# An attention and MLP block on one core: the softmax maxima turned on VectorE, a max product in the filling's bank, a constant lead and idle products in the tail

## The chip, the core and the metric

The kernel runs on one core of a Trainium2 chip. Its engines work beside each other: TensorE (PE in the profile, with its weight loads as PEld), VectorE (DVE), ScalarE (ACT), GpSimd (POOL), and SyncE (SP), which issues most of the transfers. The time is device microseconds of one execution; of the kernel before there are three runs and one profiled execution.

## The reference, cut to what matters

A transformer block with modulation by a condition vector: layer norm, attention of 32 query heads over one shared key and value head (S = 2048, D = 512, Dh = 16), a gated residual, a second layer norm and a gelu MLP (F = 1376) with another gated residual.

```python
mod = (silu(c) @ w_mod).reshape(1, 6, 1, -1)
sa, ca, ga, sb, cb, gb = (mod[:, i] for i in range(6))
h = layernorm(x) * (1 + ca) + sa
q = heads(h @ wq); k = h @ wk; v = h @ wv          # 32 heads of q, one k, one v
p = softmax(q @ k.T * Dh ** -0.5)
x = x + ga * ((p @ v) @ wo)
h = layernorm(x) * (1 + cb) + sb
x = x + gb * (gelu(h @ w1 + b1) @ w2 + b2)
```

The softmax is taken with the row maximum subtracted; all inputs are float32.

## The kernel before, in words

**Tiles.** The 2048 rows are 8 blocks of 256 rows. A block has 8 units of 4 heads, so there are 64 units. The 4 heads of a unit lie in two groups of 64 rows of the array (s = 0 and 1), two heads (j = 0 and 1) in each.

**Two passes.** Every unit's scores are computed twice. In the max pass (class `Max`) a product m of 64 x 128 queries with 512 keys goes to one of three PSUM banks (tag "m"), and VectorE reduces it to its maximum (L455); 32 of these make a unit. When the last is done, a further reduce (L463) gives the maxima mm, 128 queries by 8. Two ticks or more later `put_max` turns mm with a TensorE transpose (L475) into one more use of tag "m", ScalarE copies it to SBUF (L479), GpSimd splits it in two parts mh and ml (lines L117 and L122, in the helper `split`), and four small DMAs write these parts as two more rows of the unit's query tile qst (`send`). In the exp pass (`sexp`) the product e of keys and qst has the maximum subtracted by those rows, and ScalarE takes the exponential (L506). It needs one of four banks: e0, e1, e2, or "x". `pv` multiplies the exponentials by v into the unit's accumulator (acc, L517): 16 matmuls of the trace for one call.

**Order.** The instructions' order on each engine is the order in which the program issues them, written out by hand. The main loop runs over units u and, in each, over K = 0, 2, 4, 6. One such iteration has two half-steps, and each ends with one `pv`: 512 half-steps in all. A half-step issues four max products and four exp products and, if there is any, filling work: a half of a batch of the matmuls of other stages (late query projections, the output projection and MLP of the block before). Filling accumulates in bank "x" (its matmuls have the helper lines L165 and L171). If there is none, `plain` issues the half-step (called unfilled below; 84 of the 512). In an unfilled half-step the four exp products have the banks 1, 2, 0 and x, in the order `(K, 0, a)`, `(K, 0, b)`, `(K, 1, c)`, `(K, 1, d)` of their arguments; on TensorE the order comes out as m, m, e (bank 1), e (2), m, e (x), e (0), m. `holder` says that a batch that isn't finished holds "x"; no unfilled half-step has one.

**Due times.** `clock` counts four ticks for an iteration (one ahead of each `due()`); `later(n, fn)` issues fn at the `due()` n ticks on. `lead` says how many max products shall be done by each unit: 6 iterations' worth ahead (LEAD), and from 3 (LEAD_0) up to that over the first 8 units, which puts ten max products in place of eight into six of the early iterations.

**The rest of a block.** `rest` and `rest_steps` issue what follows a block's attention: the output projection (wops), add to x (L680), statistics (L687), normalization, transposes (tp2), modulation, the two MLP matmuls (w1ps, w2ps) and gelu. For seven blocks it is filling, for the last one (`fast`) it is the tail.

Of the kernel before, what the change touches and what calls it, by code (L numbers as in the profile page):

```python
# [9 lines left out]
F32 = mybir.dt.float32  # L10
# [12 lines left out]
LEAD = 6  # L23
LEAD_0 = 3
# [8 lines left out]
AHEAD = 0.75  # L33

# [6 lines left out]
def adaln_mqa_mlp(  # L41
# [189 lines left out]
    load_x(3)  # L231
    qbufs = [att.tile([P, 2, HQ], F32R, name=f"qst{i}") for i in range(QBUFS)]
# [191 lines left out]
    class Max:  # L424
# [17 lines left out]
        def step(self, s):  # L442
# [7 lines left out]
            m = psum.tile([P, 512], F32, name=f"m{u}_{j}_{t}_{kc}_{s}", tag="m", bufs=3)  # L450
# [9 lines left out]
            if self.left[u] == 0:  # L460
                put_at[u] = clock[0] + 2
                mm = att.tile([P, 4 * T], F32, name=f"mm{u}", tag="mm", bufs=2)
                nc.vector.tensor_reduce(out=mm, in_=self.mx.pop(u), axis=AX.X, op=ALU.max)  # L463
                maxima[u] = mm

    maxima = {}

    def put_max(u):

        w = blocks[units[u][0]][1]  # L470
        T = w // P
        qst = qsts[u]
        mm = maxima.pop(u)
        pt = psum.tile([P, 512], F32, name=f"mt{u}", tag="m", bufs=3)
        nc.tensor.transpose(pt[:4 * T, :P], mm, ident)  # L475
# [3 lines left out]
        nc.scalar.copy(m32, pt[:4 * T, :P])  # L479
# [13 lines left out]
    def sexp(u, K, j, s, bank):  # L493

        w = blocks[units[u][0]][1]
        qst = qsts[u]
        if (u, K) not in ptiles:
            ptiles[u, K] = att.tile([P, 2, 2, 512], F32, name=f"p{u}_{K}", tag="p", bufs=3)
# [21 lines left out]
    def finish_unit(u):  # L520
# [13 lines left out]
        if b == len(blocks) - 1:  # L534
# [56 lines left out]
    def rest(b, fast):  # L591
# [55 lines left out]
        ready = {}  # L647
        w1ts = {}
        later(*((5, lambda: norm(0)) if fast else (2, fetch)))
        return rest_steps(b, fast, rp, bank, ons, ready, w1ts)  # L650

    def rest_steps(b, fast, rp, bank, ons, ready, w1ts):
# [6 lines left out]
        for hf in range(w // HQ):  # L659
# [3 lines left out]
            x1 = rp.tile([P, 2, D], F32, name=f"x1_{b}_{hf}", tag="x1", bufs=2)  # L663
            xh = rp.tile([P, 2, D], F32, name=f"xh2_{b}_{hf}", tag="xh2", bufs=1)
            nc.sync.dma_start(out=x1, in_=xf[row0 + hf * HQ:row0 + (hf + 1) * HQ, :].rearrange("(t p) d -> p t d", p=P))
# [649 lines left out]
```

## Time and profile before

| | us |
|---|---|
| median of three runs | 1652.74 |
| lowest and highest | 1651.8, 1653.97 |
| the profiled execution, its own time | 1652.54 |
| its span in the trace | 1650.7 |
| PE busy | 1607.0 (97%) |
| DVE busy | 1418.3 (86%) |
| ACT busy | 1222.0 (74%) |
| POOL busy | 609.1 (37%) |

The granted TensorE clock was 0.995 in the mean. The span leaves out 1.84 us around it. Busy time of PE holds what a matmul waits inside its queue, so the shares say less than the single rows do: in a row of the timeline stand the start, the busy time, engine, line, operation, output and inputs with their shapes, how many instructions the row groups, and in brackets the idle time ahead of it and what released it.

### The profile page before, as it was taken

To read this page: it belongs to the slowest core of one execution; us is meant where nothing else is said; L and a number is where in the kernel's file an instruction comes from. 1 tells how busy PE (TensorE), PEld (TensorE's weight loads), DVE (VectorE), ACT (ScalarE), POOL (GpSimd) and SP (SyncE) were. 2 spreads that over 40 slices of the span, in tenths; PEclk is the share of its full clock that TensorE was granted. 3 is DMA by queue.
4 is the path that set the end of the run, shared out by engine and by line. 5 is a ranking of instruction groups with operands and counts; after the bars stand their busy time and mean duration, and the time that the engine had idled before them with its cause. 6 is when DMAs were issued, how large, how long until landed. Compare 5 with 4: busy or idle time off the path is not lost.

```text
span 1650.7 us, 41301 instructions
## 1 busy us (share of the span) xinstructions
PE 1607.0 (97%) x16371; PEld 1028.5 (62%) x16371; DVE 1418.3 (86%) x2433; ACT 1222.0 (74%) x2445; POOL 609.1 (37%) x894
## 2 busy tenths in 40 slices
PE   6999999999999999999999999999999999999988
PEld 4455644456666676656666576656766576656657
DVE  7788999999988998899988998999988998899524
ACT  4356777778877887778877787778877787778843
POOL 6235246424611363124601363124601363124702
PEclk9999999999999999999999999999999999999998
DMA  7244321212112130212112030212112030122122
GB/s 263 80 121 159 130 75 53 86 38 77 57 49 75 28 105 15 78 46 80 57 47 76 28 107 16 64 58 81 54 45 78 30 108 15 49 80 87 52 107 92
DMA packets 80157, 121.59 MB, mean 74 GB/s; under 512 B 15497, under 2 KB 53001, under 8 KB 79965
## 3 DMA queue, kind: packets, MB, share of 16 engines
q1 hardware_dynamic: 79852, 118.96, 22.0%
q8 instruction: 129, 2.11, 0.5%
q14 instruction: 64, 0.52, 0.1%
q0 software_dynamic: 112, 0.01, 0.0%
HBM read 91.13 MB, written 27.26 MB: 72 GB/s over the span
## 4 chain that ended last, share of the span: by engine, by line
PE 85%; DVE 8%; issue 2%; ACT 1%; DMA 1%; POOL 1%; SPq 0%; DVEq 0%; POOLq 0%; ACTq 0%
PE acc L517 29%; PE m L452 25%; PE e L505 15%; PE w1ps L171 6%; DVE mx L455 6%; PE w2ps L171 3%; PE w1ps L165 1%; PE w2ps L165 1%; PE wops L171 1%; ACT p L506 1%; PE mt L475 1%; PE kps L147 1%; PE qps L171 1%; PE tp L171 1%; DVE st L687 1%
## 5 line engine op out<-in xcount | busy, mean ns | idle before, releaser
L455 DVE TENSOR_REDUCE mx<-m 128x1 f32<-128x512 f32 x2048 | 1279.4, 683 | 145.9 <-PE m L452 115.1
L506 ACT ACTIVATE p<-e 128x512 f32<-128x512 f32 x2048 | 1070.7, 599 | 292.6 <-PE e L505 223.8
L452 PE MATMUL m<-ks,qst 64*128 64x512 f32 x2048 | 838.3, 433 | 12.8 <-DVE mx L455 4.2
L505 PE MATMUL e<-qst,ks 64*128 64x512 f32 x2048 | 700.3, 399 | 2.7 <-DMA qst<-ml 2.6
L517 PE MATMUL acc<-p,va 128*32 128x256 f32 x8192 | 548.0, 385 | 0.0
L452 PEld LDWEIGHTS m<-ks,qst 64*128 64x128 f32 x2048 | 358.6, 183 | 274.7 <-DVE mx L455 181.5
L505 PEld LDWEIGHTS e<-qst,ks 64*128 64x128 f32 x2048 | 359.0, 184 | 41.4 <-ACT p L506 19.3
L517 PEld LDWEIGHTS acc<-p,va 128*32 128x32 f32 x8192 | 213.8, 109 | 218.8 <-issue 116.7
L171 PE MATMUL w1ps<-h2H,w1t 64*128 64x256 f32 x1232 | 235.1, 287 | 0.0
L117 POOL TENSOR_SCALAR mh<-m 8x128 fp32r<-8x128 f32 x64 | 18.4, 288 | 450.7 <-ACT m L479 448.8
L171 PEld LDWEIGHTS w1ps<-h2H,w1t 64*128 64x128 f32 x1232 | 184.1, 185 | 0.0
L171 PE MATMUL w1ps<-h2L,w1t 64*128 64x256 f32 x616 | 169.5, 275 | 0.0
L171 PE MATMUL w2ps<-w2H,gL 64*128 64x512 f32 x282 | 115.7, 410 | 0.0
L171 PE MATMUL w2ps<-w2L,gH 64*128 64x512 f32 x282 | 115.5, 410 | 0.0
L171 PE MATMUL w2ps<-w2H,gH 64*128 64x512 f32 x282 | 115.3, 409 | 0.0
L171 PEld LDWEIGHTS w1ps<-h2L,w1t 64*128 64x128 f32 x616 | 113.6, 184 | 0.0
L780 POOL TENSOR_SCALAR tt<-tt 128x256 f32<-128x256 f32 x77 | 31.2, 405 | 177.2 <-DVE mx L455 96.3
L122 POOL TENSOR_TENSOR gL<-z,gH 128x256 fp32r<-128x256 f32 x88 | 66.0, 750 | 20.0 <-DVE gH L121 13.6
L781 POOL TENSOR_TENSOR tt<-tt,z 128x256 f32<-128x256 f32 x77 | 56.7, 737 | 6.4
L791 POOL TENSOR_TENSOR z<-tt,z 128x256 f32<-128x256 f32 x77 | 56.2, 729 | 6.0
L790 POOL TENSOR_TENSOR tt<-tt,z 128x256 f32<-128x256 f32 x77 | 56.2, 730 | 0.0
L171 PEld LDWEIGHTS w2ps<-w2H,gH 64*128 64x128 f32 x282 | 52.0, 184 | 0.6
(183 smaller groups left out, 1443.6 us busy)
## 6 DMA issues: line engine op xcount, KB each, us to landing
w1t<-dw SPq DMA_DIRECT2D x82, 512.0 KB
qst<-dq SPq DMA_DIRECT2D x384, 32.0 KB
do<-oc SPq DMA_DIRECT2D x64, 128.0 KB
dw<-w1s SPq DMA_DIRECT2D x11, 512.0 KB
xt<-in_A_x_dram SPq DMA_DIRECT2D x4, 1024.0 KB
wml<-in_w_mod_dram SPq DMA_DIRECT2D x8, 512.0 KB
dq<-qH SPq DMA_DIRECT2D x16, 256.0 KB
dq<-qL SPq DMA_DIRECT2D x16, 256.0 KB
```

The lines of the kernel that those rows point to most:

```text
L122: eng_l.tensor_tensor(out=dst_l, in0=src, in1=raw(dst_h), op=ALU.subtract)
L165: nc.tensor.matmul(ps, a, b_, start=first_, stop=last_)
L171: nc.tensor.matmul(ps, a[rows], b_[rows], start=first_ and s == 0, stop=last_ and s == 1)
L452: nc.tensor.matmul(m, qsts[u][rows, j, t * P:(t + 1) * P], ks[rows, kc * 512:(kc + 1) * 512], start=True, stop=True)
L455: nc.vector.tensor_reduce(out=self.mx[u][:, i, kc:kc + 1], in_=m, axis=AX.X, op=ALU.max)
L505: nc.tensor.matmul(e, ks[rows, kt * P:(kt + 1) * P], rhs, start=True, stop=True)
L506: nc.scalar.activation(ptiles[u, K][:, j, s, :], e, AF.Exp, scale=0.25)
L517: nc.tensor.matmul(accs[u][32 * cidx:32 * cidx + 32, :], va[:, kt, :], rhs, start=kt == 0, stop=kt == NKT - 1)
L780: nc.gpsimd.tensor_scalar(out=tt, in0=tt, scalar1=1.0, scalar2=1.0, op0=ALU.mult, op1=ALU.add)
L781: nc.gpsimd.tensor_tensor(out=tt, in0=tt, in1=z, op=ALU.mult)
L790: nc.gpsimd.tensor_tensor(out=tt, in0=tt, in1=z, op=ALU.mult)
L791: nc.gpsimd.tensor_tensor(out=z, in0=tt, in1=z, op=ALU.add)
```

## The change

What it does, part by part:

- **Maxima.** At a unit's last max product VectorE reduces into one of two constant tiles `mms` of 128 x 32 (zeroed at the start), and turns it with four transposes of 32 x 32 into mt (32 x 128). GpSimd's split reads mt one tick later, and the four DMAs are issued three ticks after the last maximum (`MAX_WAIT`). TensorE's transpose, ScalarE's copy and `put_some` go; 64 of each.
- **Unfilled half-steps.** `plain` puts the last max product of the row group t into bank "x", and the exp products have the banks 1, 2, 0, 1 (first half-step) and 2, 0, 1, 2 (second).
- **Lead.** 3 iterations' worth, without a ramp.
- **Loads.** x and the first three tiles of w1 of the last block are loaded by `fetch_rest` at the end of its last unit but one; for other blocks where they were. Statistics, normalization and what follows come one tick later.
- **Tail.** `stir` issues 4, 8 and 4 idle products of 128 x 512 into "x" ahead of the transposes of the second layer norm and the modulation.

```diff
-LEAD = 6
-LEAD_0 = 3
+LEAD = 3
+MAX_WAIT = (1, 3)
+STIR = (4, 8, 4)
...
+    mms = [const.tile([P, 32], F32, name=f"mm{i}") for i in range(2)]
+    for mm in mms:
+        nc.gpsimd.memset(mm, 0.0)
...
-        def step(self, s):
+        def step(self, s, **place):
             u = self.at[s]
             if u not in self.items:
                 self.begin(u)
...
             j, t, kc = self.items[u][s].pop(0)
             if not self.items[u][s]:
                 self.at[s] += 1
-            m = psum.tile([P, 512], F32, name=f"m{u}_{j}_{t}_{kc}_{s}", tag="m", bufs=3)
+            m = psum.tile([P, 512], F32, name=f"m{u}_{j}_{t}_{kc}_{s}", **(place or dict(tag="m", bufs=3)))
             rows = slice(64 * s, 64 * s + 64)
             nc.tensor.matmul(m, qsts[u][rows, j, t * P:(t + 1) * P], ks[rows, kc * 512:(kc + 1) * 512],
                              start=True, stop=True)
...
             if self.left[u] == size[u] // 2 and u and u + 1 < NU:
                 load_q(u + 1)
             if self.left[u] == 0:
-                put_at[u] = clock[0] + 2
-                mm = att.tile([P, 4 * T], F32, name=f"mm{u}", tag="mm", bufs=2)
-                nc.vector.tensor_reduce(out=mm, in_=self.mx.pop(u), axis=AX.X, op=ALU.max)
-                maxima[u] = mm
-    maxima = {}
-    def put_max(u):
-        w = blocks[units[u][0]][1]
-        T = w // P
+                put_max(u, self.mx.pop(u))
+    placed = set()
+    def put_max(u, mx):
+        T = blocks[units[u][0]][1] // P
         qst = qsts[u]
-        mm = maxima.pop(u)
-        pt = psum.tile([P, 512], F32, name=f"mt{u}", tag="m", bufs=3)
-        nc.tensor.transpose(pt[:4 * T, :P], mm, ident)
+        mm = mms[u % 2]
+        nc.vector.tensor_reduce(out=mm[:, :4 * T], in_=mx, axis=AX.X, op=ALU.max)
+        mt = att.tile([32, P], F32, name=f"mt{u}", tag="mt", bufs=2)
+        for g in range(0, P, 32):
+            nc.vector.transpose(out=mt[:, g:g + 32], in_=mm[g:g + 32, :])
         mh = att.tile([4 * T, P], F32R, name=f"mh{u}", tag="mh", bufs=2)
         ml = att.tile([4 * T, P], F32R, name=f"ml{u}", tag="ml", bufs=2)
-        m32 = att.tile([4 * T, P], F32, name=f"m32_{u}", tag="m32", bufs=2)
-        nc.scalar.copy(m32, pt[:4 * T, :P])
-        split(mh, ml, m32, nc.gpsimd, nc.gpsimd)
         def send():
             for s in range(2):
                 for r, src in ((48, mh), (49, ml)):
                     dst = qst[64 * s + r:64 * s + r + 1].rearrange("p j (t n) -> p (j t) n", n=P)
                     nc.sync.dma_start(out=raw(dst), in_=raw(src[2 * T * s:2 * T * (s + 1), :].unsqueeze(1)))
-        later(2, send)
+            placed.add(u)
+        later(MAX_WAIT[0], lambda: split(mh, ml, mt[:4 * T], nc.gpsimd, nc.gpsimd))
+        later(MAX_WAIT[1], send)
...
+            if Q == NQ - 2:
+                assert stage[b - 1] == 1
+                later(2, lambda: fetch_rest(b))
...
+    def fetch_w1(b, w1ts, f):
+        w1ts[f] = wts_pool["rest"].tile([P, 2, KD, P], F32R, name=f"w1t{b}_{f}", tag="w1t", bufs=3)
+        nc.sync.dma_start(out=raw(w1ts[f]), in_=dw1[f])
+    def fetch_rest(b):
+        row0, w = blocks[b]
+        x1 = wts_pool["rest"].tile([P, 2, D], F32, name=f"x1_{b}", tag="x1", bufs=2)
+        nc.sync.dma_start(out=x1, in_=xf[row0:row0 + w, :].rearrange("(t p) d -> p t d", p=P))
         w1ts = {}
-        later(*((5, lambda: norm(0)) if fast else (2, fetch)))
-        return rest_steps(b, fast, rp, bank, ons, ready, w1ts)
-
-    def rest_steps(b, fast, rp, bank, ons, ready, w1ts):
+        for f in range(3):
+            fetch_w1(b, w1ts, f)
+        early[b] = x1, w1ts
+    def stir(n):
+        ps = psum.tile([P, BQ], F32, name=f"stir{len(idles)}", tag="x")
+        idles.append(ps)
+        for _ in range(n):
+            nc.tensor.matmul(ps, ks[:, 0:P], ks[:, 0:BQ], start=True, stop=True)
...
-            x1 = rp.tile([P, 2, D], F32, name=f"x1_{b}_{hf}", tag="x1", bufs=2)
+            if b not in early:
+                fetch_rest(b)
+            x1, w1ts = early[b]
...
-                    later(2, lambda t=t: stats(t))
+                    later(3, lambda t=t: stats(t))
             if not fast:
-                later(3, lambda: rstd(0, 2))
-                later(4, lambda: xhat(0))
-                later(4, lambda: xhat(1))
-                yield 7
+                later(4, lambda: rstd(0, 2))
+                later(5, lambda: xhat(0))
+                later(5, lambda: xhat(1))
...
+                    stir(STIR[t])
                     for dp in range(KD // 2):
                         turn2(dp, tps[dp], t)
                     if t == 0:
                         yield LN_WAIT
+                stir(STIR[2])
                 for dp in range(KD // 2):
                     modulate(dp, tps[dp])
                 yield MOD_WAIT
...
-    for u in range(NQ):
-        lead[u] = min(first[1] + 4 * LEAD_0 + (lead[NQ] - first[1] - 4 * LEAD_0) * u / NQ, first[u + QBUFS - 1] - 2)
...
                 other = maxes(t, n)
+                if not holder and mp.has(t) and n > 1:
+                    other[-1] = 1.0, lambda: mp.step(t, tag="x", bufs=1)
                 issue(one, other[:1] + exps(t, [(K, 0, b_), (K, 1, d)]) + other[1:])
...
-                free = ((1, 2, 0, 1), (2, 0, 1, 2)) if holder else ((1, 2, 0, "x"), (1, 2, 0, "x"))
-                plain(1, X, 0, (n + 2) // 4, free[0])
+                plain(1, X, 0, (n + 2) // 4, (1, 2, 0, 1))
...
-                plain(1, Y, 0, n // 4, free[1])
+                plain(1, Y, 0, n // 4, (2, 0, 1, 2))
```

More of the change, by code (lines that the diff above doesn't have):

```diff
@@ L496, in sexp @@
         qst = qsts[u]
+        assert u in placed
         if (u, K) not in ptiles:
@@ L799, in rest_steps @@
                 if f not in w1ts:
[L800 removed]
+                    fetch_w1(b, w1ts, f)
                 w1t = w1ts.pop(f)
@@ L809, in rest_steps @@
                     if f + 3 < NF:
-                        later(1, lambda f=f: fetch_w1(f + 3))
+                        later(1, lambda f=f: fetch_w1(b, w1ts, f + 3))
             stage[b] = 1
@@ L1162, in adaln_mqa_mlp @@
             clock[0] += 1
-    for u in sorted(maxima):
-        put_max(u)
     preps["w1"] = prep_w1()
```

19 lines of the change are left out of this document (5 added, 14 removed).

## The prediction

> **What bounds the kernel now.** I read the page first (busy shares, costliest groups), then the timeline of an unfilled and of a filled half-step, then the groups by line and the tail. The page, of the kernel before:
>
> ```profile
> PE 1607.0 (97%) x16371; PEld 1028.5 (62%) x16371; DVE 1418.3 (86%) x2433; ACT 1222.0 (74%) x2445; POOL 609.1 (37%) x894
> ...
> L455 DVE TENSOR_REDUCE mx<-m 128x1 f32<-128x512 f32 x2048 | 1279.4, 683 | 145.9 <-PE m L452 115.1
> ```
>
> TensorE is never long idle, but its busy time holds waits of parts of a microsecond, which end on VectorE or ScalarE. They show only inside a half-step (of the 512 there are, 84 issue no filling work). An unfilled one, in the timeline (start, busy, engine, line, operation, and the idle before it with its releaser):
>
> ```profile
> 288.25 0.19 PEld L452 LDWEIGHTS m<-ks,qst 64*128 64x128 f32 x2 [0.41 <-DVE mx L455]
> ...
> 288.78 2.48 DVE L455 TENSOR_REDUCE mx<-m 128x1 f32<-128x512 f32 x4 [0.22 <-PE m L452]
> ...
> 289.01 2.06 ACT L506 ACTIVATE p<-e 128x512 f32<-128x512 f32 x4 [0.26 <-PE e L505]
> ...
> 289.53 0.18 PEld L452 LDWEIGHTS m<-ks,qst 64*128 64x128 f32 x1 [0.52 <-DVE mx L455]
> ...
> 289.95 0.59 PEld L517 LDWEIGHTS acc<-p,va 128*32 128x32 f32 x16 [0.24 <-issue]
> ...
> 290.95 0.19 PEld L452 LDWEIGHTS m<-ks,qst 64*128 64x128 f32 x2 [0.41 <-DVE mx L455]
> ```
>
> Call the first load T. It lasts 290.95 - 288.25 = 2.70 us. The fourth max product (289.53, T+1.28) waits for the first maximum to free one of three banks; 0.42 later the 16 acc products start, and 1.00 later the next half-step. So VectorE sets the length, although it idles 0.22 itself. The first exponential starts at T+0.76, and four take 2.06, 0.515 each. A filled one:
>
> ```profile
> 703.50 0.18 PEld L452 LDWEIGHTS m<-ks,qst 64*128 64x128 f32 x1 [0.41 <-DVE mx L455]
> ...
> 704.03 2.48 DVE L455 TENSOR_REDUCE mx<-m 128x1 f32<-128x512 f32 x4 [0.42 <-PE m L452]
> ...
> 704.26 2.11 ACT L506 ACTIVATE p<-e 128x512 f32<-128x512 f32 x4 [0.79 <-PE wops L171]
> ...
> 704.91 0.18 PEld L505 LDWEIGHTS e<-qst,ks 64*128 64x128 f32 x1 [0.17 <-ACT p L506]
> ...
> 705.35 0.59 PEld L517 LDWEIGHTS acc<-p,va 128*32 128x32 f32 x16 [0.25 <-issue]
> ...
> 706.35 0.18 PEld L452 LDWEIGHTS m<-ks,qst 64*128 64x128 f32 x1 [0.41 <-DVE mx L455]
> ```
>
> 2.85 us. Here the fourth exp product has the first one's bank, and is loaded at T+1.41, when the first exponential (T+0.76 to T+1.28) has ended; acc follows 0.44 later. ScalarE's first exponential sets the length, and VectorE has 0.42 to spare.
>
> **The change part by part.** Against the profiled run: 1652.54, 0.2 below the median.
>
> *Unfilled half-steps.* Before, the third exp product has the filling's bank and waits for nothing. After, it has bank 1 again (2 in the second half), the bank of the half-step's first exp product; the fourth max product gets the filling's bank instead. On TensorE's order the new sequence is m, m, e, e, m, e (third), e (fourth), m (fourth). So the wait for a maximum at T+1.28 goes, and one for the first exponential comes, with the last exp and the last max product queued behind it. By the two blocks above: load of the third e at 0.76 + 0.515 + 0.13 = T+1.40; the fourth max product uses the same rows of the array and comes 0.23 later; acc 0.42 after that, at T+2.05; next half-step at T+3.05. 84 x (3.05 - 2.705) = +29.0. Bounds: if only the filled half's gate bites, 84 x (2.85 - 2.705) = +12; if neither bites, VectorE's 2.48 is the length, 84 x (2.48 - 2.705) = -18.9; above, a whole exponential more, 84 x 0.515 = +43. I take +29.0, since the filled row shows this very wait.
>
> *Transposes of TensorE go.* Groups by line:
>
> ```profile
> L475 PE MATMUL mt<-ident,mm 128*8 128x128 f32 x64 | 17.5, 273 | 0.0
> ...
> L479 ACT COPY m<-mt 8x128 f32<-8x128 f32 x64 | 16.3, 255 | 30.8 <-PE mt L475 30.7
> ...
> L463 DVE TENSOR_REDUCE mm<-mx 128x8 f32<-128x32 f32 x64 | 11.9, 186 | 2.2
> ```
>
> They stand at the head of a half-step, and ahead of all that bounds it. The timeline has one, and before it a half-step with two more VectorE operations:
>
> ```profile
> 708.68 0.68 DVE L680 TENSOR_TENSOR x<-wops,x 128x512 f32<-128x512 f32 x1
> ...
> 709.25 0.18 PEld L452 LDWEIGHTS m<-ks,qst 64*128 64x128 f32 x1 [0.41 <-DVE mx L455]
> ...
> 709.28 0.68 DVE L455 TENSOR_REDUCE mx<-m 128x1 f32<-128x512 f32 x1
> ...
> 710.00 0.19 DVE L463 TENSOR_REDUCE mm<-mx 128x8 f32<-128x32 f32 x1
> ...
> 710.10 0.68 DVE L687 BATCH_NORM_STATS2 st<-x 128x6 f32<-128x512 f32 x1
> ...
> 712.85 0.08 PEld L475 LDWEIGHTS mt<-ident,mm 128*8 128x8 f32 x1 [0.41 <-DVE mx L455]
> ...
> 715.90 0.18 PEld L452 LDWEIGHTS m<-ks,qst 64*128 64x128 f32 x1 [0.41 <-DVE mx L455]
> ```
>
> 712.85 to 715.90 is 3.05, 0.20 over 2.85: 64 x 0.20 = -12.8. The ScalarE copy that goes (64 of 0.26) lies in ScalarE's idle time: 0. If VectorE hid it anyway, 0; this is the smaller end.
>
> *VectorE's new work.* Per unit the maxima's own reduce (0.186, and it starts 0.03 after the reduce it reads has ended, 710.00 against 709.28 + 0.68, where independent ones overlap by 0.08) and four transposes of 32x32. No row shows a transpose. Nearest in size is that reduce, 0.186, and the next operation starts 0.10 after it (710.10). Whether transposes overlap so is open. Where VectorE's operands change to other partitions it doesn't overlap:
>
> ```profile
> 53.83 0.68 DVE L352 TENSOR_TENSOR ks<-kps,ks 16x512 fp32r<-16x512 f32 x1 [1.99 <-ACT vt L351]
> ...
> 54.54 0.23 DVE L366 COPY va<-vps 128x64 f32<-128x64 f32 x1
> ...
> 54.68 1.88 DVE L455 TENSOR_REDUCE mx<-m 128x1 f32<-128x512 f32 x3
> ```
>
> The copy starts 0.03 after the whole of the operation before it. Each transpose reads 32 other partitions, so I take 0.186 + 0.03 = 0.22 (bounds 0.10 and, by the copy, 0.26). The unit's load is 0.11 + 0.22 + 4 x 0.22 = 1.2, of which 0.11 was there before: 1.09 more in the half-step in which the maxima end. What does that cost TensorE? The half-step from 709.25 lasted 3.60, 0.75 over, with an add and a statistic ending in it and the reduce, 1.41 of VectorE's time more than a plain one; so TensorE feels what exceeds some 0.66. A bare unit then pays 0.43; where a gelu operation, an add or a store falls in the same half-step, 0.75 to 0.83 (the gelu's, by its row, 0.40 from start to start).
> ```profile
> 592.38 0.48 DVE L775 TENSOR_SCALAR z<-w1ps,b1c 128x256 f32<-128x256 f32 x1
> 592.78 0.68 DVE L455 TENSOR_REDUCE mx<-m 128x1 f32<-128x512 f32 x1
> ```
>
> Over the eight units of a block that is 4.2 (mostly bare ones, and two or three of the others), seven blocks 29.6, and 2.2 for the first units: +32. With 0.10 each: +12.
>
> By the Trainium skill ("VectorE: DVE Perf Modes", section "Two Vector instructions with no wait between them") a Vector instruction whose first input begins in another group of 32 partitions than the last one read from that memory waits until all earlier ones have finished. It calls this a model; the row at 54.54 agrees with it. By that rule three of the four transposes are held, and the sum is the one below; without it the sum is rival A's.
>
> *Lead and waits.* The constant lead of 3 takes away two extra max products in each of six early iterations, four filled (eight halves) and two unfilled:
>
> ```profile
> 174.04 0.18 PEld L452 LDWEIGHTS m<-ks,qst 64*128 64x128 f32 x1 [0.41 <-issue]
> ...
> 177.34 0.18 PEld L452 LDWEIGHTS m<-ks,qst 64*128 64x128 f32 x1 [0.41 <-DVE mx L455]
> ...
> 267.69 0.19 PEld L452 LDWEIGHTS m<-ks,qst 64*128 64x128 f32 x2 [0.41 <-DVE mx L455]
> ...
> 271.81 0.19 PEld L452 LDWEIGHTS m<-ks,qst 64*128 64x128 f32 x2 [0.41 <-DVE mx L455]
> ```
>
> A filled half with five products lasted 3.30 (8 x 0.45 = -3.6), an unfilled one with six 4.12, of which 0.2 is the reduce of a unit's maxima that falls in it (two, 1.2 each above 2.705: -2.4). The twelve are done in the last unit but one, where no max work was left and exponentials set the pace: 0, at most +6. The early, ramped lead also let two exp products wait for their maxima:
>
> ```profile
> 113.67 0.29 POOL L117 TENSOR_SCALAR mh<-m 8x128 fp32r<-8x128 f32 x1
> ...
> 117.81 0.47 PE L505 MATMUL e<-qst,ks 64*128 64x512 f32 x1 [1.30 <-DMA qst<-ml]
> ```
>
> Two of these go: -2.6. From the split on GpSimd to the released product are 4.14 us. After, the maxima end in the second half of a unit's third iteration (start T0); the split can begin at about T0+3.0, and the rows are there at T0+7.2. The next unit needs them three half-steps after T0, at T0+8.6 or later: 1.4 to spare. Four small DMAs on SP are as many as before; no load stands ahead of them at that place. The statistics put off by one tick no longer share the half-step of the add (709.28): seven blocks, 0.75 each, -5.2; at least 0, if the new work takes the same place.
>
> *Tail.*
>
> ```profile
> 1600.21 0.43 SPq L665 DMA_DIRECT2D x<-in_A_x_dram  x1
> ...
> 1604.30 0.69 DVE L680 TENSOR_TENSOR x<-wops,x 128x512 f32<-128x512 f32 x1 [4.51 <-DMA x<-in_A_x_dram]
> ...
> 1616.00:1618.00 2.00, 2.00 (x11) 2.00 (x11) 0.42 (x1) 0.78 (x2) 0.00 (x0) 0.50 0.49 131
> 1618.00:1620.00 2.00, 2.00 (x14) 2.00 (x13) 0.43 (x1) 1.15 (x3) 0.00 (x0) 0.65 0.60 203
> ```
>
> (The last two are the windows of the trace; the column after POOL is the granted clock.) The load that VectorE waits 4.51 for is issued a unit earlier. It took 4.09 from its issue, which is the most that can go; the product that it is added to is not ready at once either, and I take 2.5. The clock of 0.5 in these 2 us costs about 1, of 0.65 about 0.7; 16 idle products should hold it, and cost nothing where TensorE waits: -2. Together -4.5, between 0 and -6; above, +3 if the idle products stand in the way.
>
> Sum: +29.0 - 2.4 - 12.8 + 32 - 3.6 - 2.6 - 5.2 - 4.5 = +29.9, so 1682.
>
> **The rivals.** *A: transposes overlap* at 0.10 each. For it: small VectorE operations in the trace do. Against: the partitions change. +12 in place of +32: 1662.
> *B, the other side: the third e's wait doesn't decide.* If the first exponential ends by the time the third e is reached, the fourth bank for maxima frees VectorE: 2.48 in place of 2.705, 1682 - 29.0 - 18.9 = 1634. It decides if the e loads later than the 1.28 of the old wait by nothing, that is with the first exponential over by T+1.15; the trace has T+1.28. Half of it (filled length, +12) with A is 1645.
> *C: the short lead is too short,* and the next unit's e waits for ml as in the rows at 117.81: 1.3 in some 50 filled units, +65: 1747. Against it are the 1.4 us of margin.
>
> **How the numbers follow.** What this kernel's measurement can tell from no change is about 0.2%, 1649.4 to 1656.0. Likeliest, as summed: 0.57 (own range 1668 to 1692, from the transposes' 0.16 to 0.26 and a tail of 0 to -6). A, or halfway to it: 0.21, of which 0.04 within 0.2% (with +12 for the unfilled steps). B: 0.16, of which 0.14 faster and 0.02 within 0.2%. C: 0.06. B and C outside make 0.2: range 1652 to 1695. Faster 0.14, same 0.06, slower 0.80.
>
> **What would show it.** Right: unfilled half-steps of about 3.05, the third e with idle time released by ACT p; four transposes that start about 0.22 apart; the half-step in which a unit's maxima end about 3.3; no e that waits for ml; no 4.51 wait before the add in the tail and a granted clock near 1.0. Wrong: unfilled half-steps of 2.5 or 2.85, transposes 0.1 apart, or idle time of e released by a DMA.

## The result, and the profile after

The changed kernel takes 1706.17 us (median of four runs, 1705.26 to 1707.07), before it is 1652.29 in the same comparison: 1.0324 times as long, with a 95% interval of 1.0306 to 1.0342. The prediction had the direction, with 1682 and a range that ended at 1695. It had slightly over half of the loss.

The page of the changed kernel, busy time and costliest groups (line numbers have moved: L452 is L456, L455 is L459, L505 is L509, L506 is L510, L517 is L521, L463 is L476, L171 is L172 and L775 is L800; in the kernels of the experiments they move by a few lines again):

```profile
PE 1620.9 (95%) x16323; PEld 1020.1 (60%) x16323; DVE 1470.0 (86%) x2689; ACT 1222.0 (72%) x2381; POOL 610.6 (36%) x896
L459 DVE TENSOR_REDUCE mx<-m 128x1 f32<-128x512 f32 x2048 | 1275.9, 679 | 152.6 <-PE m L456 128.9
...
L479 DVE STREAM_TRANSPOSE mt<-mm 32x32 f32<-32x32 f32 x256 | 51.3, 200 | 7.3 <-DVE mm L476 0.5
```

VectorE has 51.3 us more to do, the 256 transposes, and the span is 53.9 longer. That the two are alike is chance: the terms are larger, and of both signs. An unfilled half-step in the timeline:

```profile
288.53 0.19 PEld L456 LDWEIGHTS m<-ks,qst 64*128 64x128 f32 x2 [0.41 <-DVE mx L459]
...
289.07 2.48 DVE L459 TENSOR_REDUCE mx<-m 128x1 f32<-128x512 f32 x4 [0.59 <-PE m L456]
289.31 2.27 ACT L510 ACTIVATE p<-e 128x512 f32<-128x512 f32 x4 [0.81 <-PE e L509]
289.95 0.19 PEld L509 LDWEIGHTS e<-qst,ks 64*128 64x128 f32 x2 [0.89 <-ACT p L510]
...
290.62 0.59 PEld L521 LDWEIGHTS acc<-p,va 128*32 128x32 f32 x16 [0.37 <-issue]
291.62 0.19 PEld L456 LDWEIGHTS m<-ks,qst 64*128 64x128 f32 x2 [0.41 <-DVE mx L459]
```

From 288.53 to 291.62 are 3.09 us. The third exp product is loaded at T+1.42, released by ScalarE's exponential, and acc follows at T+2.09: the wait that the prediction put there, at its place. VectorE now idles 0.59 in place of 0.22. The half-step in which a unit's maxima end, and the next one, with gelu work as filling:

```profile
624.59 0.19 DVE L476 TENSOR_REDUCE mm<-mx 128x8 f32<-128x32 f32 x1
624.60 0.59 PEld L521 LDWEIGHTS acc<-p,va 128*32 128x32 f32 x16 [0.24 <-issue]
...
624.82 0.84 DVE L479 STREAM_TRANSPOSE mt<-mm 32x32 f32<-32x32 f32 x4
625.59 0.64 DVE L459 TENSOR_REDUCE mx<-m 128x1 f32<-128x512 f32 x1
625.60 0.18 PEld L456 LDWEIGHTS m<-ks,qst 64*128 64x128 f32 x1 [0.41 <-issue]
...
626.26 0.48 DVE L800 TENSOR_SCALAR z<-w1ps,b1c 128x256 f32<-128x256 f32 x1
626.66 3.07 DVE L459 TENSOR_REDUCE mx<-m 128x1 f32<-128x512 f32 x5
626.80 0.18 PEld L172 LDWEIGHTS w1ps<-h2H,w1t 64*128 64x128 f32 x1 [0.91 <-DVE z L800]
...
629.64 0.18 PEld L456 LDWEIGHTS m<-ks,qst 64*128 64x128 f32 x1 [0.41 <-issue]
```

The half-step from 625.60 lasts 4.04 us. TensorE's first filling product (626.80) waits for z, the operation that reads the filling's bank and so frees it; z stands in VectorE's queue behind the reduce of the maxima, the four transposes and one more reduce.

The main loop's half-steps can be paired one to one with those before, since both kernels fill the same ones (a half-step is counted from the start of its 16 acc products to that of the next):

| half-steps | count | us before | us after | difference |
|---|---|---|---|---|
| unfilled, no transposes in them | 59 | 161.2 | 181.4 | +20.2 |
| unfilled, with VectorE's transposes | 19 | 56.4 | 66.8 | +10.4 |
| filled, with VectorE's transposes | 44 | 127.7 | 165.9 | +38.3 |
| filled, in which TensorE's transpose was | 56 | 170.7 | 160.2 | -10.5 |
| of the iterations with ten products before, eight after | 12 | 41.7 | 35.6 | -6.0 |
| other filled | 316 | 921.1 | 923.6 | +2.5 |
| in the last unit but one, where the twelve products that went from above now lie | 4 | 11.5 | 11.6 | +0.1 |

That is +54.9. The stretch ahead of the first acc is 3.0 longer (96.4 to 99.4), the one behind the last half-step 4.0 shorter (63.3 to 59.3).

The prediction named an exp product that waits for ml as a sign of being wrong. There are two, for 1.7 us in all, as many as before but at other places. This is the row of the waits (who waits, for what, us in all, times, longest):

```profile
PE e L509 <- DMA qst<-ml: 1.7, 2, 1.0
```

### The profile page after: what moved, and what is told of

Same layout as the page of the kernel before. It is cut to its first block, busy times and chain, and to the rows that moved or that the text cites. A ratio compares the mean times of both kernels' runs of the same rounds, so it can differ in the third digit from the quotient of the medians.

```text
span 1704.6 us, 41437 instructions
## 1 busy us (share of the span) xinstructions
PE 1620.9 (95%) x16323; PEld 1020.1 (60%) x16323; DVE 1470.0 (86%) x2689; ACT 1222.0 (72%) x2381; POOL 610.6 (36%) x896
## 4 chain that ended last, share of the span: by engine, by line
PE 82%; DVE 10%; ACT 3%; issue 2%; DMA 1%; POOL 0%; SPq 0%; DVEq 0%; POOLq 0%; ACTq 0%
PE acc L521 27%; PE m L456 23%; PE e L509 16%; PE w1ps L172 6%; DVE mx L459 6%; PE w2ps L172 3%; ACT p L510 3%; DVE mt L479 2%; PE wops L172 2%; PE w2ps L166 1%; PE w1ps L166 1%; PE qps L172 1%; PE kps L148 1%; DVE z L800 1%; PE qps L166 1%
## 5 line engine op out<-in xcount | busy, mean ns | idle before, releaser
L459 DVE TENSOR_REDUCE mx<-m 128x1 f32<-128x512 f32 x2048 | 1275.9, 679 | 152.6 <-PE m L456 128.9
L510 ACT ACTIVATE p<-e 128x512 f32<-128x512 f32 x2048 | 1089.0, 597 | 354.8 <-PE e L509 282.2
L456 PE MATMUL m<-ks,qst 64*128 64x512 f32 x2048 | 842.4, 433 | 8.6 <-DVE mx L459 8.0
L509 PE MATMUL e<-qst,ks 64*128 64x512 f32 x2048 | 718.8, 407 | 34.9 <-ACT p L510 31.4
L521 PE MATMUL acc<-p,va 128*32 128x256 f32 x8192 | 548.0, 385 | 0.0
L456 PEld LDWEIGHTS m<-ks,qst 64*128 64x128 f32 x2048 | 359.9, 184 | 265.8 <-DVE mx L459 155.0
L509 PEld LDWEIGHTS e<-qst,ks 64*128 64x128 f32 x2048 | 349.7, 185 | 100.3 <-ACT p L510 78.4
L521 PEld LDWEIGHTS acc<-p,va 128*32 128x32 f32 x8192 | 213.8, 109 | 231.1 <-issue 124.5
L172 PE MATMUL w1ps<-h2H,w1t 64*128 64x256 f32 x1232 | 240.9, 291 | 6.4 <-DVE z L800 6.4
L118 POOL TENSOR_SCALAR mh<-mt 8x128 fp32r<-8x128 f32 x64 | 18.5, 289 | 568.3 <-DVE mt L479 568.3
L172 PEld LDWEIGHTS w1ps<-h2H,w1t 64*128 64x128 f32 x1232 | 186.4, 186 | 12.5 <-DVE z L800 12.4
L172 PE MATMUL w1ps<-h2L,w1t 64*128 64x256 f32 x616 | 171.7, 279 | 0.0
L172 PE MATMUL w2ps<-w2H,gH 64*128 64x512 f32 x282 | 116.1, 412 | 3.0 <-DVE z L800 2.9
L172 PE MATMUL w2ps<-w2L,gH 64*128 64x512 f32 x282 | 117.0, 415 | 0.0
L172 PE MATMUL w2ps<-w2H,gL 64*128 64x512 f32 x282 | 116.3, 412 | 0.0
L172 PEld LDWEIGHTS w1ps<-h2L,w1t 64*128 64x128 f32 x616 | 114.7, 186 | 0.0
L479 DVE STREAM_TRANSPOSE mt<-mm 32x32 f32<-32x32 f32 x256 | 51.3, 200 | 7.3 <-DVE mm L476 0.5
```

The source lines that it names most:

```text
L172: nc.tensor.matmul(ps, a[rows], b_[rows], start=first_ and s == 0, stop=last_ and s == 1)
L456: nc.tensor.matmul(m, qsts[u][rows, j, t * P:(t + 1) * P], ks[rows, kc * 512:(kc + 1) * 512], start=True, stop=True)
L459: nc.vector.tensor_reduce(out=self.mx[u][:, i, kc:kc + 1], in_=m, axis=AX.X, op=ALU.max)
L479: nc.vector.transpose(out=mt[:, g:g + 32], in_=mm[g:g + 32, :])
L509: nc.tensor.matmul(e, ks[rows, kt * P:(kt + 1) * P], rhs, start=True, stop=True)
L510: nc.scalar.activation(ptiles[u, K][:, j, s, :], e, AF.Exp, scale=0.25)
```

## The experiments

### Undoing the two parts

Three kernels, each from the changed one. The banks and the place of the last max product as before:

```diff
-                if not holder and mp.has(t) and n > 1:
-                    other[-1] = 1.0, lambda: mp.step(t, tag="x", bufs=1)
...
-                plain(1, X, 0, (n + 2) // 4, (1, 2, 0, 1))
+                plain(1, X, 0, (n + 2) // 4, (1, 2, 0, 1) if holder else (1, 2, 0, "x"))
...
```

> The changed kernel with the banks of the unfilled half-steps as before: all max products in the three banks of their own, the third exp product in the filling's bank. Theory (the third exp product waits for the first exponential, 0.36 us in each of 84 unfilled half-steps): unfilled half-steps go from 3.07 back to 2.71, some 30 us are won, 1676. Rival (the wait there is only the place where VectorE's extra work shows): unfilled half-steps stay at 3 us, 1700 to 1706.

Measured: 1694.89 us (in brackets, here and below, the ratio to the kernel before and its 95% interval: 1.0255, 1.0238 to 1.0272). A win of 11 us, where 30 was expected. Unfilled half-steps without transposes are back at 2.70 to 2.71 us, 0.365 less, as the theory says; in the trace they won 17 us in all. But the 19 with transposes went the other way, 7 us longer together. One of them, in the timeline of this kernel:

```profile
255.37 0.19 PEld L456 LDWEIGHTS m<-ks,qst 64*128 64x128 f32 x2 [0.41 <-DVE mx L459]
...
256.01 0.84 DVE L479 STREAM_TRANSPOSE mt<-mm 32x32 f32<-32x32 f32 x4
256.79 2.43 DVE L459 TENSOR_REDUCE mx<-m 128x1 f32<-128x512 f32 x4
...
257.48 0.18 PEld L456 LDWEIGHTS m<-ks,qst 64*128 64x128 f32 x1 [1.36 <-DVE mx L459]
...
258.90 0.19 PEld L456 LDWEIGHTS m<-ks,qst 64*128 64x128 f32 x2 [0.41 <-DVE mx L459]
```

3.53 us, where the changed kernel has 3.07 for the same half-step. With three banks the fourth max product has to wait 1.36 for VectorE, with the filling's bank as a fourth it does not. So the fourth bank, even with the wait that it brings, is 0.3 to 0.5 better in the half-steps with the transposes, where VectorE is late, and 0.365 worse where it isn't. The two parts of the change are not independent, and the theory had treated them so.

TensorE's transpose and ScalarE's copy in place of the four transposes:

```diff
...
-        for g in range(0, P, 32):
-            nc.vector.transpose(out=mt[:, g:g + 32], in_=mm[g:g + 32, :])
+        def turn_maxima():
+            pt = psum.tile([P, 512], F32, name=f"mt{u}", tag="m", bufs=3)
+            nc.tensor.transpose(pt[:4 * T, :P], mm[:, :4 * T], ident)
+            nc.scalar.copy(mt, pt[:4 * T, :P])
+            split(mh, ml, mt, nc.gpsimd, nc.gpsimd)
...
+        later(MAX_WAIT[0], turn_maxima)
```

> The changed kernel with the maxima turned by TensorE and copied by ScalarE as before (at the next tick), not by four VectorE transposes. Theory (the transposes hold up what frees the filling's bank: 44 filled half-steps pay 0.87 us, 19 unfilled ones 0.45): some 47 us go, 11.5 us for TensorE's transposes come back, 1670. Rival (the loss in these half-steps is from the short lead and the wait of the next unit's exp products for the maxima): 1700 or more.

Measured: 1687.12 (1.0209, 1.0193 to 1.0224), a win of 19. The half-steps that had the transposes got 41 (filled), 8 (unfilled) and, where unit ends meet other stages, 6 us shorter: the 47 or more that the theory gives them. But the transpose on TensorE cost 37 in place of 11.5. In the timeline of the kernel with both parts undone:

```profile
610.82 0.19 DVE L476 TENSOR_REDUCE mm<-mx 128x8 f32<-128x32 f32 x1
...
611.05 0.08 PEld L481 LDWEIGHTS mt<-ident,mm 128*8 128x8 f32 x1 [0.48 <-DVE mm L476]
```

Issued one tick after the last maximum, it stands ahead of the acc products and waits for the reduce that it reads. The kernel before has it a half-step later.

The two edits together:

> Both of these undone at once; what is left of the change is the constant lead, the early loads, the later ticks and the idle products in the tail. Theory: the two costs add up, 1640, which is faster than the kernel before by some 12 us. Rival (they share the 19 unfilled half-steps with transposes, or the lead itself costs): 1648 to 1655.

Measured: 1665.24 (1.0076, 1.0058 to 1.0094), slower than expected by 25. Most of this is that same wait: 0.41 in each of 59 filled half-steps, 24 us where TensorE's transposes were to cost 11.5, and 8 in five unfilled ones; the rest was not taken apart. So this kernel doesn't show what is left of the change when both parts are undone. That took two more steps:

```diff
-        later(MAX_WAIT[0], turn_maxima)
+        later(2, turn_maxima)
```

> As e3_both, but TensorE's transpose issued one tick later, behind the acc products, when the reduce it reads has long ended. Theory (in e3_both TensorE waits for that reduce, 0.41 a filled half-step and over 1 an unfilled one): half of 24 us and nearly all of 13 go, 1642, faster than the kernel before by some 10 us, from the constant lead, the tail and the waits at the early units. Rival (the later turn makes the next unit's exp products wait for the maxima, with a lead of 3): 1690 or more.

Measured: 1747.18 (1.0578, 1.0551 to 1.0606): the rival. The timeline and the windows of this kernel (the column after POOL's busy time is the granted clock):

```profile
600.15 0.29 POOL L118 TENSOR_SCALAR mh<-m 8x128 fp32r<-8x128 f32 x1
...
604.27 0.76 PE L513 MATMUL e<-qst,ks 64*128 64x512 f32 x1 [2.22 <-DMA qst<-ml]
```

```profile
602.00:604.00 2.00, 0.04 (x1) 0.00 (x0) 0.78 (x2) 0.01 (x1) 1.81 (x3) 0.92 0.01 3
604.00:606.00 2.00, 1.73 (x11) 1.76 (x12) 0.50 (x1) 0.60 (x1) 1.77 (x3) 0.50 0.80 272
606.00:608.00 2.00, 2.00 (x15) 1.41 (x16) 1.09 (x3) 1.41 (x3) 0.10 (x1) 0.50 0.24 67
608.00:610.00 2.00, 2.00 (x19) 0.88 (x13) 0.48 (x1) 0.70 (x3) 0.00 (x0) 0.50 0.15 33
610.00:612.00 2.00, 2.00 (x24) 1.72 (x26) 1.66 (x3) 1.61 (x5) 0.00 (x0) 0.87 0.19 66
```

From the split to the product are 4.12 us, as in the kernel before. The turn comes so late that TensorE stands still for 2.2 us at the head of a unit, and then works for more than 6 us at half its clock. The waits of this kernel (engine and line, releaser: us in all, times, longest) have 29 such products:

```profile
PE e L513 <- DMA qst<-ml: 54.5, 29, 2.9
```

This is the prediction's rival C, in another kernel: a short lead has no room for one tick more.

One iteration more of lead:

```diff
-LEAD = 3
+LEAD = 4
```

> As e10_pe_turn2, with a constant lead of 4 in place of 3. Theory (in e10_pe_turn2 the next unit's exp products wait 2.2 us for the maxima, and run at a lower granted clock after it: 101 us in the filled first half-iterations): one iteration more, 5.7 us, covers the wait, all of it goes, less some 3 us for more max products ahead of the loop: 1647. Rival (the transposes at the head of the half-step cost what e3_both showed): 1665.

Measured: 1680.87 (1.0175, 1.0159 to 1.0190). The waits for ml are nearly gone (seven, 4.0 us in all, where 29 had 54.5), but the unit's last max product now falls at the end of a half-step, and the transpose, at the head of the next, waits again. The view of the waits of this kernel:

```profile
PEld mt L481 <- DVE mm L476: 66.7, 64, 1.9
```

### The order within an unfilled half-step

```diff
-                issue(one, other[:1] + exps(t, [(K, 0, b_), (K, 1, d)]) + other[1:])
+                e_b, e_d = exps(t, [(K, 0, b_), (K, 1, d)])
+                issue(one, other[:1] + [e_b] + other[1:] + [e_d])
```

> The changed kernel with the order in an unfilled half-step changed alone: the exp product that uses a bank again comes last, behind the max product in the filling's bank. Theory: it waits as long as before (to T+1.40) but nothing is queued behind it but the acc products, so the half-step is as long as a filled one, 2.85: 84 x 0.22 = 18 us won, 1688. Rival (VectorE decides once it has the fourth bank): 2.5 us, 1658. No change (1706) if the wait is not what sets the length.

Measured: 1692.88 (1.0247, 1.0232 to 1.0262), 13 us won. Unfilled half-steps without transposes are 2.84 us long, 0.23 less, as expected; 61 x 0.23 = 14. Those with transposes stay, which had been counted in. So of the 0.365 that the other banks cost, 0.23 is what is queued behind the third exp product, and some 0.13 (2.84 against 2.71) stays with the wait itself.

### What a transpose costs, and where it stands

Four more transposes per unit that all read the same 32 rows:

```diff
+        spare = att.tile([32, P], F32, name=f"spare{u}", tag="spare", bufs=2)
+        for g in range(0, P, 32):
+            nc.vector.transpose(out=spare[:, g:g + 32], in_=mm[0:32, :])
```

> The changed kernel with four more transposes of 32x32 per unit behind the four, into a tile that nobody reads; the four more all read the same 32 rows. Theory 1 (a transpose is held when its input begins in other rows than the last read, and takes 0.21 from start to start then): the sixth to eighth start about 0.1 after the one before, the unit's four more take some 0.5 us, and where VectorE's time there is paid in full by TensorE, 63 x 0.5 = 32 us more: 1738. Theory 2 (a transpose takes 0.21 from start to start in any case): 0.85 us, 1760. Rival (TensorE waits for something else than VectorE in these half-steps): 1706 to 1715.

Measured: 1740.35 (1.0519, 1.0501 to 1.0538), 34 us more than the changed kernel.

```profile
638.24 0.84 DVE L479 STREAM_TRANSPOSE mt<-mm 32x32 f32<-32x32 f32 x4
639.11 0.48 DVE L482 STREAM_TRANSPOSE spare<-mm 32x32 f32<-32x32 f32 x4
639.53 0.64 DVE L459 TENSOR_REDUCE mx<-m 128x1 f32<-128x512 f32 x1
```

The four that read other rows each time take 0.84 us together, the four on the same rows 0.48. Over all units the median from start to start is 0.213 for the first kind, and for the last two of the second kind 0.093. That is what the Trainium skill's page "VectorE: DVE Perf Modes" says in its section "Two Vector instructions with no wait between them": an instruction whose first input begins in another group of 32 partitions than the last one read is held until the earlier ones have finished. The page calls it a model; these rows agree with it, and 0.12 us of each transpose is that.

The 34 us are the number of the theory, but not for its reason: the extra 0.5 us on VectorE is not paid in full. In the profiled execution (1745.76), whose main loop is 38 us longer than the changed kernel's, the 63 half-steps with transposes are 26 longer: 0.36 to 0.50 each in most of them, and nothing in the five unfilled ones in which VectorE has no other work. Another 15 us are in unfilled half-steps without transposes, most of them just behind one with them, where the granted clock falls to 0.50. Three windows of this kernel at such a place, and the changed kernel's at the same work (the granted clock again behind POOL's busy time):

```profile
363.00:365.00 2.00, 1.39 (x7) 0.61 (x7) 2.00 (x5) 1.18 (x3) 0.00 (x0) 1.00 0.01 2
365.00:367.00 2.00, 2.00 (x20) 0.97 (x20) 2.00 (x4) 0.99 (x2) 0.00 (x0) 0.60 0.06 18
367.00:369.00 2.00, 1.74 (x7) 0.85 (x6) 2.00 (x6) 1.09 (x2) 1.24 (x3) 0.50 0.16 45
```

```profile
361.00:363.00 2.00, 2.00 (x23) 0.90 (x21) 2.00 (x4) 1.22 (x3) 0.00 (x0) 1.00 0.03 9
363.00:365.00 2.00, 1.55 (x20) 0.71 (x19) 2.00 (x6) 1.91 (x4) 1.18 (x3) 1.00 0.18 45
```

The transposes one tick later, nothing else:

```diff
-        for g in range(0, P, 32):
-            nc.vector.transpose(out=mt[:, g:g + 32], in_=mm[g:g + 32, :])
+        def turn(a, b):
+            for g in range(a, b, 32):
+                nc.vector.transpose(out=mt[:, g:g + 32], in_=mm[g:g + 32, :])
...
+        later(MAX_WAIT[0], lambda: turn(0, P))
```

> The changed kernel with the four transposes issued one tick later, behind the VectorE operations of the half-step in which the maxima end (so behind the one that frees the filling's bank), and nothing else moved. Theory (what is lost over 0.42 in the filled half-steps is the wait of the filling's first product for that operation): the 44 go from 0.87 to 0.42, 20 us won, 1686. Rival (all VectorE time is paid where it stands): no change, 1706.

Measured: 1685.64 (1.0197, 1.0182 to 1.0212), the number that was expected.

```profile
621.02 0.19 DVE L476 TENSOR_REDUCE mm<-mx 128x8 f32<-128x32 f32 x1
621.13 0.68 DVE L459 TENSOR_REDUCE mx<-m 128x1 f32<-128x512 f32 x1
621.73 0.48 DVE L803 TENSOR_SCALAR z<-w1ps,b1c 128x256 f32<-128x256 f32 x1
622.03 0.18 PEld L456 LDWEIGHTS m<-ks,qst 64*128 64x128 f32 x1 [0.41 <-DVE mx L459]
...
622.72 0.83 DVE L481 STREAM_TRANSPOSE mt<-mm 32x32 f32<-32x32 f32 x4
...
625.60 0.18 PEld L456 LDWEIGHTS m<-ks,qst 64*128 64x128 f32 x1 [0.41 <-DVE mx L459]
```

The same operations in another order: z comes ahead of the transposes, the filling's first product waits no more, and the half-step from 622.03 lasts 3.57 in place of 4.04. So part of the 47 us is not VectorE's time as such, but what stands behind it. The theory put all 20 us into the 44 filled half-steps; in the trace these won 15, and 8 came from unfilled ones, where the transposes have left the half-step of an add or a modulation (3.71 and 3.65 to 3.08 us). There max products wait for reduces of earlier ones, and no filling is held up. That the sum comes out is luck in part.

One transpose at each of four ticks, with the lead at 4:

```diff
-LEAD = 3
-MAX_WAIT = (1, 3)
+LEAD = 4
+MAX_WAIT = (4, 6)
...
+        later(1, lambda: turn(0, 32))
+        later(2, lambda: turn(32, 64))
+        later(3, lambda: turn(64, 96))
+        later(4, lambda: turn(96, 128))
```

> The changed kernel with the four transposes issued one at each of the next four ticks, two in a half-step, and the lead at 4 in place of 3 so that the maxima are still there in time. Theory (VectorE has 0.42 to spare in each half-step, and a transpose takes 0.21): the transposes cost next to nothing, 47 us less 0 to 10: 1660 to 1668. Rival (each transpose pays its 0.2 wherever it stands, as it holds up the next reduce): 64 x 0.6, about as the changed kernel, 1695 or more.

Measured: 1676.95 (1.0145, 1.0130 to 1.0161). The main loop is 36 us shorter than the changed kernel's, so at least 11 of the 47 remain, and the longer lead costs 6 ahead of the loop. Two things were changed at once here: the longer lead also ends waits for late maxima (4 us, see below), so what the spread transposes cost by themselves is not shown more closely. Spread work is cheaper, but not free.

The later transposes and the banks of before, the two edits shown above together:

> The transposes one tick later as in e7_turn_late, and the banks of before as in e1_banks. Theory (e1_banks won 0.365 in each unfilled half-step that has no transposes, but lost 0.3 to 0.4 where VectorE has the transposes, as there the fourth bank helps): 1685.6 less 22 to 24, plus 8: 1671. Rival (the two costs stand apart): 1655.

Measured: 1676.92 (1.0148, 1.0134 to 1.0161): 9 us won over the later transposes alone, far nearer to the theory's 1671 than to 1655.

### The tail

```diff
-STIR = (4, 8, 4)
+STIR = (0, 0, 0)
...
```

> The changed kernel without the idle products. Theory (they hold the granted clock in the stretch of LN and transposes): the clock falls to 0.5 to 0.65 for 2 to 4 us again and the stretch behind the last half-step is 1.5 to 2 us longer, 61 in place of 59.3. Rival (they stand in TensorE's way or do nothing): 58.5 to 59.5.

Measured: 1708.55, in one execution alone, so only its trace says something: the stretch behind the last half-step is 61.15 us, against 59.29 with the idle products. Windows of it, and of the changed kernel:

```profile
1670.00:1672.00 2.00, 1.99 (x9) 1.69 (x9) 0.03 (x1) 0.49 (x2) 0.73 (x1) 0.50 0.00 0
```

```profile
1670.00:1672.00 2.00, 1.69 (x13) 1.48 (x13) 0.09 (x1) 0.84 (x2) 0.57 (x1) 1.00 0.00 2
```

A clock of 0.50 without them, 1.00 with them: 1.9 us by the idle products, and the other 2.2 (63.34 to 61.15) by the earlier loads.

And the kernel before with this part alone:

```diff
+            if Q == NQ - 2:
+                assert stage[b - 1] == 1
+                later(2, lambda: fetch_rest(b))
...
+                    stir(STIR[t])
...
+                stir(STIR[2])
...
```

> The kernel before with the tail's part of the change alone: the last block's x and first w1 tiles loaded a unit earlier, and the 4, 8 and 4 idle products. Theory: the 4.0 us by which the stretch from the last main half-step on is shorter in the changed kernel (63.3 to 59.3) come from these, 1648.5. Rival (they come from the other order of the last unit): 1652 to 1653.

Measured: 1648.87 (0.9976, 0.9968 to 0.9985), as expected.

### The terms that were to win

The last one with the later statistics:

```diff
-                    later(2, lambda t=t: stats(t))
+                    later(3, lambda t=t: stats(t))
...
-                later(3, lambda: rstd(0, 2))
-                later(4, lambda: xhat(0))
-                later(4, lambda: xhat(1))
-                yield 7
+                later(4, lambda: rstd(0, 2))
+                later(5, lambda: xhat(0))
+                later(5, lambda: xhat(1))
+                yield 8
```

> e12_tail with the statistics and what follows them one tick later, as in the change. Theory (in the changed kernel the half-step of the add lost its 0.6, but a half-step some units on, where x is normalized, got 0.5 longer): the 5 us of the prediction do not come, 1648 to 1650. Rival (they do, and the longer half-step has another cause): 1644.

Measured: 1643.76 (0.9947, 0.9935 to 0.9959): the rival, and the prediction's own term. Seven half-steps of the add go from 3.60 to 3.02, seven unfilled ones lose 0.6 and their successors gain 0.5; the main loop is 5.2 us shorter. So in the changed kernel those 5 us came too, and something else took them back. Its timeline at the head of unit 20, one of the seven half-steps that got 0.55 longer:

```profile
577.99 0.54 DVE L753 TENSOR_SCALAR h<-tp,cb,sb 128x256 f32<-128x256 f32 x1
...
578.62 0.41 POOL L118 TENSOR_SCALAR h2H<-h 128x256 fp32r<-128x256 f32 x1 [0.60 <-DVE h L753]
579.11 0.73 POOL L123 TENSOR_TENSOR h2L<-h,h2H 128x256 fp32r<-128x256 f32 x1
579.82 0.29 POOL L118 TENSOR_SCALAR mh<-mt 8x128 fp32r<-8x128 f32 x1
...
583.91 0.18 PEld L509 LDWEIGHTS e<-qst,ks 64*128 64x128 f32 x1 [0.37 <-issue]
```

The split of the maxima stands in GpSimd's queue behind the split of the normalized x (h2H, h2L), which had itself waited 0.60 for VectorE's modulation (L753), and that stands behind the four transposes. The first exp product is loaded 4.09 after the split of the maxima, about as long as the rows at 600.15 and 113.67 show for this chain. With a lead of 3 that is too late by half a microsecond. The profile calls the wait "issue", so that it is the maxima is argued from the times, not shown by a releaser; these half-steps last 3.5 to 3.6 in the changed kernel, 3.0 in the kernel with TensorE's turn and a lead of 4, and 2.9 in the one with TensorE's turn alone, whose lead is 3; in the one with both parts undone, where the half-steps ahead of them are shorter, they last 3.5 again.

The changed kernel with the banks of before and:

```diff
-LEAD = 3
-MAX_WAIT = (1, 3)
+LEAD = 4
+MAX_WAIT = (1, 6)
...
+        later(4, turn_maxima)
```

> The changed kernel with the banks of before, TensorE's transpose four ticks after the last maximum, its DMAs six after it, and a constant lead of 4. Theory (e11_pe_turn2_lead4 lost 41 us in the half-steps at whose head the transpose waits for the reduce of the maxima, as that reduce stands behind the gelu's operation and the last max): the wait goes, what stays is the lead's gain of 8.6 less some 3 ahead of the loop, and the tail: 1643, faster than before. Rival (the turned maxima come too late, or the transpose waits again): 1660 or more.

Measured: 1646.93 (0.9961, 0.9949 to 0.9973). With TensorE's transpose four ticks after the last maximum it waits for the reduce of the maxima at one unit alone, for 1.9 us, and two exp products wait 0.7 for ml; this kernel is 0.4% faster than the one before. It is not faster than the one with the tail and the later statistics alone: its main loop is 2.7 us shorter, its start 2.8 longer.

And the kernel with the tail's part alone, with a constant lead:

```diff
-LEAD = 6
+LEAD = 5
...
-    for u in range(NQ):
-        lead[u] = min(first[1] + 4 * LEAD_0 + (lead[NQ] - first[1] - 4 * LEAD_0) * u / NQ, first[u + QBUFS - 1] - 2)
```

> e12_tail with a constant lead of 5 without a ramp, and nothing else. Theory (no half-steps with ten products, no early waits for maxima: -8.6; 12 to 16 more products ahead of the loop, some 6 us, from the prologue of e11_pe_turn2_lead4): 1646. Rival (the products ahead of the loop cost as much as is won): 1649 or more.

Measured: 1661.11 (1.0052, 1.0040 to 1.0064), past the rival. The start is 9.4 us longer for the larger lead, and one unit's first half-step takes 8.5 us, as its four small DMAs stand in SP's queue behind the loads of an output block (the product waits 5.4 for ml); the half-steps with ten products are gone as expected. So the lead's gain is real, and paid at the start.

## Why the prediction was right or wrong

- **The third exp product's wait** (+29.0): right in its place, its releaser and its size, 3.07 to 3.09 where 3.05 was worked out. The rival that it doesn't decide is dead. What the step lacked is that the fourth bank for maxima is 0.3 to 0.5 better in the half-steps with transposes, so that undoing it gives back 11, not 29. In the five unfilled half-steps in which VectorE has the transposes and no other work, these cost nothing at all (3.06 to 3.09 us, as without them).
- **VectorE's work** (+32): the durations were right, 0.213 against 0.22 for a transpose, and rival A with 0.10 is dead. The step that failed is what TensorE pays for them, in two places. One is "mostly bare ones, and two or three of the others": in the blocks with filling only two of eight units are bare, and six have another VectorE operation in the half-step (three a gelu's, one a store, one an add, one a modulation). With the prediction's own prices that is 0.43 x 2 + 0.79 x 6 = 5.6 per block in place of 4.2, some 41 in all, so by this reckoning 9 of the missing 15. The other is "TensorE feels what exceeds some 0.66". It holds where VectorE has nothing else (3.25 to 3.40 in filled half-steps, 0.42 to 0.56 more than before, 0.43 worked out). Where a gelu or a store falls in, 0.75 to 0.83 was predicted, and 1.0 to 1.1 (gelu: 2.85 to 3.83, 2.91 to 4.02, 2.94 to 4.05) and 1.25 (store: 3.05 to 4.30) was measured: that operation frees the bank that TensorE's next filling product needs at once (the row at 626.80; for the store the waits have PE wops released by DVE ot, six times up to 0.8 us), so there is no slack for it, and all VectorE work ahead of it is paid. The later transposes agree: with z ahead of them, 4.04 became 3.57, still 0.6 over the 2.94 of before. Together +47 (38.3 in the filled half-steps, and 66.8 - 19 x 3.07 = 8.5 in the unfilled ones) in place of +32.
- **TensorE's transposes** (-12.8): -10.5 in the filled half-steps, right.
- **The lead** (-3.6, -2.4 and -2.6): the half-steps with ten products gave 6.0, as summed, and the two early waits of 1.3 each went. Two others came in their place, 1.0 and 0.7 long. The clause "no load stands ahead of them at that place" failed at the second: at 1085.83 the small DMAs follow eight of an output block on SP, as in the last experiment.
- **The margin** of 1.4 us for the maxima: right for most units. The clause that the split "can begin at about T0+3.0" failed for one unit a block, where GpSimd's queue is full, itself held up by VectorE; 3.9 us, which took back most of the later statistics' -5.2. That this is the cause is argued, as said above.
- **The tail** (-4.5): -4.0, of which -1.9 by the idle products (-2) and -2.2 by the loads (-2.5), from one trace without the idle products. The -2 was read off two windows of 2 us; the clock of the kernel before is at 0.50 from about 1609 to 1619, so that this part fits so well is luck in part.
- **The start**: no term, and +3.0 measured. The first max product comes 1.2 later in the changed kernel, but later still, by 1.9, in the kernel with the tail's part alone, whose loop begins only 0.6 later than before: so that is not a cost of the change by itself. Three kernels of the experiments that issue the same instructions ahead of the loop as the changed one (other banks, other order, no idle products) begin it at 98.9 to 100.3 in their one trace each, so part of the 3.0 may be scatter between executions. Where the rest comes from stays open.

Term by term: 1682, plus 15 for VectorE's work behind which the filling waits, 4 for the late maxima, 3 at the start and 2 or 3 for the rest, is the 1706. The range was too narrow because the transposes' upper end moved only their duration, never the share of it that TensorE pays, nor the number of half-steps that pay more.

## What to carry to other kernels

The slack of an engine that isn't the bound is not one number for a half-step: ask for each of its instructions who waits for it, and put new work behind the one that frees a buffer for the bound engine, not ahead of it. Count also how many of the places where new work is put hold other work already. Moving four instructions by one tick was worth 20 us here. When an order is changed, the waits that replace the old one are to be priced with what is queued behind them; the kernel with the tail's loads, the idle products and the later statistics alone, 1643.76 us, is the fastest here and leaves both costly parts out.

## What the runs showed of the hardware that was not expected

TensorE's granted clock fell to 0.50 within a gap of 2.2 us without work (602.04 to 604.27 in the kernel with the late turn; a mean of 0.92 from 602 to 604 puts the fall at about 603.7), and stayed there for more than 6 us of work, to about 610.5. The half-step with this wait lasts 7.1 us in place of 2.95, 4.2 more, of which the wait is 2.2. In the kernel with eight transposes the clock fell at nine places of the main loop, 3.4 or 6.8 us each time, and in the 3.4 us ahead of none of these falls did TensorE's products leave a gap of over 0.8 us. The Trainium skill, page "TensorE: Matmul & The Clock Gate", section "What's actually happening", gives in its table of the clock's states at least one idle window of about 3.4 us for the slow state; the shorter gaps in these rows were enough. What sets the fall off at some of these places and not at others was not tried.

A VectorE transpose of 32x32 that is held takes 0.213 us from start to start, one that isn't 0.093, while their recorded durations, 0.199 and 0.157 in the median, differ by a third of that.
